# Layer two's Q and K by seven block products, one token class at a time, with the orders of four engines written out

## The chip, the cores and the metric

The kernel runs on one core of a Trainium2 chip. A core has a matrix engine (TensorE, PE in the profile), three engines that work on elements (VectorE or DVE, ScalarE or ACT, GpSimd or POOL), and a sync engine (SyncE or SP), which here issues all DMA copies. Each engine runs its own instructions in order, and an instruction that needs another engine's result waits for it; what stands behind it on the same engine waits too. Matmuls read SBUF and write PSUM, which has eight banks of 128 x 512 fp32. The metric is the device time of one execution in microseconds (us).

## The reference

Two layers, each a sliding-window attention (A) and a token-mixing MLP (B), on x of 2048 tokens x 1024 features, all in bf16:

```python
def _A_ref(x, wqkv, wo):                     # H = 32 heads of 32, W = 8, dilation 2
    qkv = ((x @ wqkv).reshape(B, S, 3, H, Dh)).transpose(2, 0, 3, 1, 4)
    q, k, v = qkv[0], qkv[1], qkv[2]
    idx = pos[:, None] - off[None, :]        # off = 0, 2, 4, ... 14
    ...
    attn = softmax(where(mask, einsum("bhsd,bhswd->bhsw", q, kg) * scale, -1e9))
    return (einsum("bhsw,bhswd->bhsd", attn, vg)...) @ wo

def _B_ref(x, w1, b1, w2, b2):
    u = gelu(einsum("bsd,sf->bdf", layernorm(x), w1) + b1)
    return (einsum("bdf,fs->bds", u, w2) + b2).transpose(0, 2, 1)

x = x + _A_ref(layernorm(x), A_wqkv, A_wo);  x = x + _B_ref(layernorm(x), ...)
x = x + _A_ref(layernorm(x), A_wqkv, A_wo);  x = x + _B_ref(layernorm(x), ...)
```

Since the dilation is 2, even and odd tokens never meet in attention. They are the two token classes, 1024 tokens each.

## The kernel before

Both layers run in one program: V for all tokens, attention with Q and K, the output projection (`out_proj`), then B's two GEMMs (`gemm1`, and `gemm2f` in layer one, `gemm2s` in layer two). In layer two, V already uses seven block products in place of eight (`Sevens`, Strassen's scheme in Winograd's form): weights and tokens are cut into 2 x 2 blocks, sums of blocks are made on DVE in fp16, and each product is four matmuls of 128 x 128 by 128 x 512 (L445). Sums between products are made by copying a PSUM bank with ACT and letting the next product add to the copy. `ahead(p, n)` hangs other work into four rounds of two token blocks each.

Attention is cut into 16 units `u` (a group of four heads, a class) and each unit into two visits of 512 tokens. Before the change both layers run the same loop (L1533): a visit issues on PE, in this order, `scores` of this visit (16 small matmuls on 32-wide tiles, one output bank for two of the four token blocks), `values` of the visit before, and two chunks of `qk_chunk` of the next unit (each 8 matmuls of 128 x 512 into an `m` bank). `in_order` fixes that order. ACT turns scores into exponentials (`pc`, L540), DVE multiplies them with the band mask into `Pm` (L552), `values` multiplies `Pm` with `v` and with ones, ACT makes the reciprocal by Ln and Exp (L588, L589), and DVE writes `oT` (L591). The keys of a unit go to `kT`; q is spread with zeros between the heads into `qB`, so that one small matmul serves four heads. ACT casts a q chunk to `qs`, and the four heads' rows go to `qB` by DVE copies (L516) or, for heads from `1 + 2n` on, by DMA from SP (L518). There are two `qB`, used in turn, and `Pm` has three slots.

The banks come from three pools: `s` has 4 banks, `m` 2 and `a` 2; scores take two `s`, values two `a`, a q or k chunk one `m`.

In the loop the weights `wqk` come in four pairs of 512 KB (`load_qk`), and in layer two DVE also takes maxima over parts of w2 (`top_load`, `top2`). `zero_p` and `zero_q` clear `Pm` and `qB` on DVE during V. In the last unit two tiles of `out_proj` a visit stand where the chunks were; a tile is two halves of 8 matmuls (L621), a residual add on DVE each (L628) with `xr`, which SP loads three ahead (`load_xr`), and the layer norm in three steps (`ln_step`).

Of the kernel before, what the change touches and what calls it, by code (L numbers as in the profile page):

```python
# [17 lines left out]
P = 128  # L18
# [10 lines left out]
def kernel(  # L29
# [135 lines left out]
    mxv = const.tile([P, 2, KD // 2], FP32, name="mxv")  # L165
    mv2 = const.tile([P, 2], FP32, name="mv2")
    csv = const.tile([P, 1], FP32, name="csv")
    civ = const.tile([P, 1], FP32, name="civ")
# [5 lines left out]
    def zero_q():  # L174
        for t in qB:
            r = nc.vector.memset(t[:].rearrange("p h t -> p (h t)"), 0.0)
        return r

    def zero_p():
        return nc.vector.memset(Pm[:].rearrange("p h t k -> p (h t k)"), 0.0)  # L180

    def zero_fill():
        zero_p()
        return zero_q()
# [4 lines left out]
    mxp = dram.tile([P, NPRE + 1], FP32, name="mxp")  # L189
    mxvd = dram.tile([P, 2], FP32, name="mxvd")  # L190
# [45 lines left out]
    def start_up(v, wv):  # L236
# [107 lines left out]
        def top_wv():  # L344
            return nc.vector.tensor_reduce(out=mv2[:], in_=mxv[:], op=ALU.max, axis=AX.X)
# [61 lines left out]
    def power_wv():  # L407
        chain_("DVE", powers, 0, 1, bcw.pop("v")[:].rearrange("p q c -> p (q c)"), csv, civ)

    class Sevens:  # L410
# [3 lines left out]
        def scale(self, j):  # L414
            w = self.wv[j][:]
            chain_("ACT", lambda: nc.scalar.activation(out=w.bitcast(FP16), in_=w, func=ACT.Identity, scale=csv[:]))
# [34 lines left out]
        def run(self, v, ahead):  # L451
# [9 lines left out]
            def put(i, r, c, src, z):  # L461
                dst = v[r][i][:, c * 512:(c + 1) * 512]
                return nc.vector.scalar_tensor_tensor(out=dst, in0=src, scalar=civ[:], in1=z, op0=ALU.mult, op1=ALU.add)

            for p in range(0, NI, 2):
# [6 lines left out]
                for i in pr:  # L472
                    in_order(self.product, bk[i][1], self.S[i][:, 0], Tn(1))
                    Z[i] = x2("z", [P, 512], FP32)
                    chain_(A, move, Z[i][:], bk[i][1], civ[:])
# [4 lines left out]
                for i in pr:  # L480
                    in_order(self.product, bk[i][0], self.a(i, 0, 1), B(1, 0), False)
                    chain_(A, move, v[0][i][:, 0:512], bk[i][0], civ[:])
# [7 lines left out]
                for i in pr:  # L490
                    in_order(self.product, bk[i][3], self.a(i, 1, 1), Tn(4), False)
                    chain_(A, move, v[1][i][:, 0:512], bk[i][3], civ[:])
# [34 lines left out]
    def scores(u, b):  # L527
        q, k = qB[u % 2], kT[u % 2]
        s0 = (2 * u + b) % NS * HB
# [8 lines left out]
        pc = pcp.tile([P, HB, HG, GW], BF16, name="pc", tag="pc")  # L538
        for n in range(2):
            nc.scalar.activation(out=pc[:, 2 * n:2 * n + 2].rearrange("p t h k -> p (t h k)"), in_=ss[n][:, 0:2 * HG * GW],  # L540
                                 func=ACT.Exp, scale=scale, bias=shift[:])
        exps[:] = pc, s0
# [3 lines left out]

    def mask(*rs):
        pc, s0 = exps
        for r in rs:
            rp = slice(r * KG, (r + 1) * KG)  # L550
            mk = band[rp].unsqueeze(1).unsqueeze(1).to_broadcast([KG, HB, HG, GW])
            mm = nc.vector.tensor_tensor(out=Pm[rp, :, s0:s0 + HB, r * KG:r * KG + GW].rearrange("p h t k -> p t h k"),  # L552
                                    in0=pc[rp], in1=mk, op=ALU.mult)
        return mm

    def values(u, b, v, oT):
        g, c = divmod(u, DIL)
# [23 lines left out]
        for lo_, n_, t_ in runs:  # L581
            for h in range(HG):
# [3 lines left out]
                                      skip_group_check=True)  # L586
        rd = x2("rd", [P, 512], FP32)
        nc.scalar.activation(out=rd[:], in_=acc[1][:], func=ACT.Ln)  # L588
        nc.scalar.activation(out=rd[:], in_=rd[:], func=ACT.Exp, scale=-1.0)  # L589
        lo = c * SC + t0 * P  # L590
        norm.append(lambda: nc.vector.tensor_tensor(out=oT[g][:, lo:lo + HB * P], in0=acc[0][:], in1=rd[:], op=ALU.mult))  # L591
        return mm

    norm = []
# [213 lines left out]
    def top_load(k):  # L808
        t = wt_("w2p", [P, 8, 256])
        pre[k] = t  # L810
        for n in range(2):
            i, f = divmod(2 * k + n, NB2)
            r = nc.sync.dma_start(out=t[:, 4 * n:4 * n + 4], in_=w2_v[:, 4 * f:4 * f + 4, i * 256:(i + 1) * 256])
        return r

    def top2(k, j):
        i, f = divmod(4 * k + j, 2 * NB2)
        return nc.vector.tensor_reduce(out=mx2[:, i, f:f + 1], in_=pre[k][:, 2 * j:2 * j + 2, :], op=ALU.max, axis=AX.XY,
                                       apply_absolute_value=True)

    pre = {}

    def gemm1(h2, g, first):
# [115 lines left out]
        for fb in range(1, NFB):  # L939
# [59 lines left out]
            if not first and fb == 2:  # L999
                share_w2(0, 2 * NB2)  # L1000
            if not first and fb == 5:
# [180 lines left out]
    def gemm2f(g, src, dst, seam):  # L1182
# [180 lines left out]
        t2(*range(4))  # L1363
        normalise(0, 1)
# [31 lines left out]
        for i in range(2, NI):  # L1396
# [55 lines left out]
            if i + 2 < NI:  # L1452
                load_w(i + 2)
                if i == 3:
# [46 lines left out]
    for li in range(2):  # L1501
        first = li == 0
        v = [[None] * NI for _ in range(DIL)]
        for c, i in order:
            v[c][i] = vhp.tile([P, D], BF16, name="v", tag="vh")
        if first:
# [3 lines left out]
            res = lambda c, i: xin_v[c, i]  # L1510
        else:
            def ahead(p, n):
                if p == 0 and n == 0:
                    rest()
                elif p == 2 and n == 0:
                    chain_("DVE", zero_p)
                elif p == 4 and n == 0:
                    chain_("DVE", zero_q)
                elif n and p + 2 < NI:
                    for m in range(4):  # L1520
                        for k in range(2):
                            sv[0].s_sum(p + 2 + k, m)

            sv[0].run(v, ahead)
            res = lambda c, i: rows(xb, c, i)
        oT = [gop.tile([P, S], BF16, name="oT", tag="go") for _ in range(NG)]
        h2 = [[None] * NI for _ in range(DIL)]
        chunks = [(0, 0), (0, 1), (1, 0), (1, 1)]
        if first:
            last_pe[0] = None  # L1530
        for part, n in chunks:
            in_order(qk_chunk, 0, wts, part, n)
        for vis in range(2 * NU):  # L1533
            u, b = divmod(vis, 2)
            if first and vis == 5:
                chain_("SP", keep_wv)
            if b == 0 and u % (2 * DIL) == 1 and u + 3 < NU:
                nxt = [None, None]
                chain_("SP", load_qk, u // (2 * DIL) + 1, nxt)
            if b == 0 and (u + 1) % (2 * DIL) == 0 and u + 1 < NU:  # L1540
                wts = nxt
            if vis == 2 * NU - 8:
                wo = []
                chain_("SP", load_wo, wo)
            if vis == 2 * NU - 3:
                todo[:] = order
                for _ in range(3):
                    load_xr(res)
            if vis % 4 == 0 and vis < 4 * (DIL * NPRE if first else NB2):
                chain_("SP", pre_load if first else top_load, vis // 4)  # L1550
            in_order(scores, u, b)
            if u + 1 < NU:
                mask(0, 1, 2, 3)
            else:
                chain_("DVE", mask, 0, 1)
            if vis:
                in_order(values, *divmod(vis - 1, 2), v, oT)
                if u + 1 < NU:
                    divided = norm.pop()()
                else:  # L1560
                    chain_("DVE", norm.pop())
            k, j = divmod(vis - 3, 4)
            if 0 <= k < (DIL * NPRE if first else NB2):
                with tc.issue_after(divided.ins):
                    (pre_top if first else top2)(k, j)
            if first and vis == 2 * NU - 4:
                bc0 = pre_share()
            for n in range(2):
                if u + 1 < NU:
                    in_order(qk_chunk, u + 1, wts, *chunks[2 * b + n])  # L1570
                    continue
                half, add, store, ln = out_proj(0, 2 * b + n, oT, wo, res, xa[li], h2)
                in_order(half, 0)
                chain_("DVE", add, 0)
                if n == 0:
                    chain_("DVE", mask, 2, 3)
                else:
                    ln_step()
                in_order(half, 1)
                chain_("DVE", add, 1)  # L1580
                store()
                lns.append(list(ln))
                if n:
                    ln_step()
        in_order(values, NU - 1, 1, v, oT)
        if first:
            chain_("DVE", power, 0, 1 + NPRE, bc0[:].rearrange("p q b -> p b q"))
        for k, (c, i) in enumerate(order[4:]):
            if k in (8, 10):
                chain_("SP", load_w1, k // 2 - 4)  # L1590
# [24 lines left out]
        wv, wts = [], [None, None]  # L1615
# [41 lines left out]
```

## Time and profile before

| | us |
|---|---|
| runs (three) | 1199.63, 1200.66, 1204.48 |
| median | 1200.66 |
| the profiled execution's own time | 1200.14 |
| its span | 1198.4 |
| layer one, attention with Q and K (PE L505) | 62.6 to 203.1 |
| layer two, V (L447) | 607.9 to 656.4 |
| layer two, attention with Q and K | 656.4 to 797.4 |
| layer two, rest of attention and output projection | 797.4 to 861 |
| layer two, first GEMM from block 1 on | about 872 to 1029 |

Busy us in three of these windows:

| window | PE | DVE | ACT | POOL | DMA, GB/s |
|---|---|---|---|---|---|
| 62.6 to 203.1 | 140.5 | 110.2 | 96.2 | 0 | 79 |
| 607.9 to 656.4 | 48.5 | 30.3 | 25.7 | 0 | 33 |
| 656.4 to 797.4 | 140.3 | 112.2 | 96.4 | 0 | 81 |

Times in a table or in a profile line are us from the start of the span; the span runs from the first to the last instruction, and the profiled execution's own time has a little more around it. In a line of the timeline the first number is the start, the second how long the group took, and `x16` the number of instructions in it; in a line of a group the last numbers are busy time and the mean of one in ns, and after the second bar the idle time before them.

### The profile page before, as it was taken

The numbers are of one execution on the slowest core, as the hardware profiler recorded it, in microseconds if no ns is written. First come the engines' busy times: TensorE is split into PE (matmuls) and PEld (weight loads), VectorE is DVE, ScalarE is ACT, GpSimd is POOL, SyncE is SP. The second block draws the span as 40 slices with busy tenths as digits, with TensorE's granted clock in tenths as the row PEclk, the third lists the DMA queues.
The fourth block names the chain that finished last, engine by engine and source line by source line (L and its number), as shares of the span: only waits on it lengthen the run. The fifth ranks groups of instructions, "written<-read, shape, count | busy, mean of one in ns | idle before, by whom it ended". The sixth has DMA issues, their size and how long they took to land.

```text
span 1198.4 us, 20518 instructions
## 1 busy us (share of the span) xinstructions
PE 1191.6 (99%) x7972; PEld 548.5 (46%) x7972; DVE 780.6 (65%) x1513; ACT 692.9 (58%) x1164; POOL 125.6 (10%) x121
## 2 busy tenths in 40 slices
PE   9999999999999999999999999999999999999998
PEld 4444444444444444444444444444444444444444
DVE  7558887887777546957665788888612221874663
ACT  5757676578777777665744677654544434432342
POOL 0000000281000031000000000003911212100000
PEclk9999999999999999999999999999999999999999
DMA  8922233696676778975510232435855645175521
GB/s 238 158 63 71 72 109 94 207 284 176 183 222 180 211 198 190 219 186 147 177 43 19 68 85 71 121 98 176 263 161 164 202 146 168 41 193 141 156 73 36
DMA packets 248561, 174.12 MB, mean 145 GB/s; under 512 B 48400, under 2 KB 224784, under 8 KB 245136
## 3 DMA queue, kind: packets, MB, share of 16 engines
q1 hardware_dynamic: 248464, 172.82, 52.3%
q8 instruction: 62, 1.02, 0.4%
q14 instruction: 35, 0.29, 0.1%
HBM read 130.30 MB, written 30.43 MB: 134 GB/s over the span
## 4 chain that ended last, share of the span: by engine, by line
PE 97%; DMA 1%; ACT 1%; DVE 0%; issue 0%; DVEq 0%
PE m L505 19%; PE s L876 11%; PE m L621 9%; PE m L876 7%; PE s L1080 7%; PE a L876 6%; PE s L1230 5%; PE m L1080 4%; PE s L297 3%; PE a L1080 3%; PE m L1230 3%; PE s L702 2%; PE s L536 2%; PE s L447 2%; PE s L1323 2%; PE a L1230 2%
## 5 line engine op out<-in xcount | busy, mean ns | idle before, releaser
L505 PE MATMUL m<-hT,wqk 128*128 128x512 bf16 x1024 | 231.8, 380 | 0.0
L552 DVE TENSOR_TENSOR Pm<-pc,band 32x640 bf16<-32x640 bf16 x256 | 123.5, 483 | 45.6 <-ACT pc L540 38.8
L505 PEld LDWEIGHTS <-wqk 128*128 128x128 bf16 x1024 | 95.3, 98 | 117.9 <-issue 10.7
L876 PEld LDWEIGHTS <-Sw 128*128 128x128 f16 x832 | 81.4, 98 | 98.7 <-issue 0.7
L621 PE MATMUL m<-wo,oT 128*128 128x512 bf16 x512 | 111.8, 379 | 0.0
L876 PEld LDWEIGHTS <-w 128*128 128x128 f16 (+1 forms) x624 | 61.1, 98 | 73.6
L716 POOL TENSOR_TENSOR T<-h 128x512 f16<-128x512 bf16 x16 | 18.4, 1152 | 606.4 <-DMA xr<-xb 357.5
L621 PEld LDWEIGHTS <-oT 128*128 128x128 bf16 x512 | 49.6, 98 | 60.6 <-issue 1.9
L716 DVE TENSOR_TENSOR py<-pz,m 128x512 f32<-128x512 f32 x14 | 9.6, 688 | 91.2 <-PE m L876 62.8
L540 ACT ACTIVATE pc<-s,shift 128x320 bf16<-128x320 f32 x128 | 60.9, 532 | 11.6 <-PE s L536 11.6
L876 PE MATMUL s<-T,Sw 128*128 128x512 f16 x288 | 66.2, 379 | 0.4 <-ACT s L885 0.4
L512 ACT CAST qs<-m 128x512 bf16<-128x512 f32 x64 | 37.5, 586 | 44.3 <-PE m L505 41.2
L509 ACT CAST kT<-m 128x512 bf16<-128x512 f32 x64 | 37.5, 586 | 41.8 <-PE m L505 38.8
L716 POOL TENSOR_TENSOR Pm<-g 128x512 f16<-128x512 bf16 x24 | 28.6, 1208 | 282.5 <-ACT Pm L797 163.7
L628 DVE TENSOR_TENSOR xn<-m,xr 128x512 bf16<-128x512 f32 x64 | 44.1, 689 | 15.2 <-PE m L621 15.0
L661 ACT ACTIVATE h<-xn,bi,rs 128x1024 bf16<-128x1024 bf16 x32 | 39.7, 1240 | 23.1 <-DVE bi L647 23.1
L876 PE MATMUL a<-h,w 128*128 128x512 bf16 x224 | 52.9, 379 | 0.0
L876 PE MATMUL m<-T,Sw 128*128 128x512 f16 x224 | 52.9, 379 | 0.0
L852 ACT ACTIVATE w<-w,cs 128x2048 f16<-128x2048 bf16 x26 | 51.8, 1997 | 0.0
L1080 PEld LDWEIGHTS <-u 128*128 128x128 f16 x336 | 32.9, 98 | 39.6
L516 DVE COPY qB<-qs 32x512 bf16<-32x512 bf16 x136 | 38.2, 281 | 18.5 <-ACT qs L512 15.5
L716 DVE TENSOR_TENSOR xs<-tq,xs 128x512 bf16<-128x512 f32 (+1 forms) x30 | 21.9, 733 | 43.2 <-ACT tq L1235 26.1
(251 smaller groups left out, 2183.6 us busy)
## 6 DMA issues: line engine op xcount, KB each, us to landing
w<-in_B_w_dram SPq DMA_DIRECT2D x110, 512.0 KB, 6.1
sd<-Sw SPq DMA_DIRECT2D x13, 1024.0 KB, 8.3
Sw<-sd SPq DMA_DIRECT2D x13, 1024.0 KB, 4.9
wqk<-in_A_wqkv_dram SPq DMA_DIRECT2D x16, 512.0 KB, 5.0
xa<-xn SPq DMA_DIRECT2D x32, 256.0 KB, 3.2
xs<-xa SPq DMA_DIRECT2D x32, 256.0 KB, 3.4
Pm<-in_B_w_dram SPq DMA_DIRECT2D x26, 256.0 KB, 6.4
wo<-in_A_wo_dram SPq DMA_DIRECT2D x8, 512.0 KB, 5.8
```

Source lines behind the costliest of these rows:

```text
L505: mm = nc.tensor.matmul(ps[:], lhsT=wts[part][:, kt, (g % 2) * P:(g % 2 + 1) * P], rhs=hT[:, kt, lo:lo + 512], start=(kt == 0), stop=(kt = ...
L516: nc.vector.tensor_copy(out=qB[u % 2][hp, h, ls], in_=qs[hp, :])
L540: nc.scalar.activation(out=pc[:, 2 * n:2 * n + 2].rearrange("p t h k -> p (t h k)"), in_=ss[n][:, 0:2 * HG * GW], func=ACT.Exp, scale=scal ...
L552: mm = nc.vector.tensor_tensor(out=Pm[rp, :, s0:s0 + HB, r * KG:r * KG + GW].rearrange("p h t k -> p t h k"), in0=pc[rp], in1=mk, op=ALU.mult)
L621: mm = nc.tensor.matmul(ps[:], lhsT=oT[g][:, cols(c, i)], rhs=wo[n][g // 4][:, g % 4, :], start=(g == 0), stop=(g == NG - 1))
L628: return nc.vector.tensor_tensor(out=xn[:, xs_], in0=pss_["o", n][:], in1=xr[:, xs_], op=ALU.add)
L661: last["ACT"] = nc.scalar.activation(out=h2[c][i][:], in_=xn[:], func=ACT.Identity, bias=t["bi"][:], scale=t["rs"][:])
L716: return eng.tensor_tensor(out=out, in0=a, in1=b, op=op)
L852: return nc.scalar.activation(out=w[:].bitcast(FP16), in_=w[:], func=ACT.Identity, scale=cs[:, fb + 1:fb + 2])
L876: r = nc.tensor.matmul(out, lhsT=lhs[:, k, :], rhs=rhs[k], start=start and k == 0, stop=stop and k == NI - 1, skip_group_check=True)
L1080: r = nc.tensor.matmul(out, lhsT=lhs[k], rhs=rhs[k][:, cols_], start=start and k == 0, stop=k == K - 1, skip_group_check=True)
L1230: r = nc.tensor.matmul(out, lhsT=lhs[k], rhs=rhs[k], start=start and k == 0, stop=k == K - 1, skip_group_check=True)
```

## The change

Layer one keeps its loop, with one addition: after every second visit ACT takes a sum of absolute values over half a `wqk` tile (`bound_qk`), 16 in all, from which a scale for the fp16 weights of Q and K follows (`mxq`, then `mv2`, `csv` and `civ`, which now have two columns). The step that sends these to DRAM (`keep_wv`) moves from layer one's attention into `gemm2f`.

Layer two gets two classes. `QkBlocks` works during V: it loads the weights of two head groups at a time (512 KB, k or q), scales them on ACT, makes the four weight sums on DVE, and writes both to DRAM (`sdq`). The clearing of `Pm` and `qB` moves from DVE to GpSimd. `Attention` then runs cycles `p` = 0 to 7, and a remainder as cycle 8. A cycle makes k and q of two head groups of one class by seven products each and does the four visits of the cycle before. All of class 0 comes first (`by_class`). Products 1 and 5 take an `s` bank each, the two banks that are copied on an `m` bank each. The order of each engine is a list; `-` means an item of the cycle before, and `cycle` only interleaves the four lists so that each item's needs come earlier.

```diff
+    def by_class(u):
+        p = u // 2
+        return 2 * (p % (NG // 2)) + u % 2, p // (NG // 2)
+    class QkBlocks:
+        def load(self, n):
...
+            chain_("SP", lambda: nc.sync.dma_start(out=self.R[n][:], in_=wq_v[:, :, lo:lo + 256]))
+        def scale(self, n):
+            t = self.R[n][:]
+            chain_("ACT", lambda: nc.scalar.activation(out=t.bitcast(FP16), in_=t, func=ACT.Identity, scale=csv[:, 1:2]))
+        def sums(self, n):
...
+            for o, x, y, op in ((q[0], a21, a22, ALU.add), (q[1], q[0], a11, ALU.subtract), (q[2], a11, a21, ALU.subtract),
+                                (q[3], a12, q[1], ALU.subtract)):
+                chain_("DVE", tt, nc.vector, o, x, y, op)
+        def keep(self, n):
...
+            chain_("SP", lambda: nc.sync.dma_start(out=sdq[n][0], in_=r[:].bitcast(FP16)))
+            chain_("SP", lambda: nc.sync.dma_start(out=sdq[n][1].rearrange("p k c -> p (k c)"), in_=t[:].rearrange("p a k c -> p (a k c)")))
+    class Attention:
+        NP = 4 * NG // 4
+        PE = "P1k P4q- P5k S1 P6k V1 P2k P7k S2 P3k V2 P4k P1q P5q S3 P6q V3 P2q P3q S4 P7q V4"
+        ACT = ("x4- abk c21q- e1a e1b pck l1 x1 Zk c11k e2a e2b l2 x2 abq c21k e3a e3b pcq l3 x3 Zq c11q e4a e4b l4")
+        DVE = ("m40- n4- m41- m42- m43- m10 m11 m12 m13 n1 y22k y12k m20 m21 m22 n2 m23 t1 m30 m31 m32 m33 n3 y12q y22q t2")
+        SP = "dc21q- wk wq dy12q dc11q dy22q"
...
+            return {"S": [("e" + o + "a", d), ("e" + o + "b", d), ("dc11q", p - 1), ("dy12q", p - 1)]
+                    + ([("dc21q", p - 1), ("dy22q", p - 1)] if c in "34" else []),
...
+        def cycle(self, p):
+            qs = {}
+            for e in ("PE", "ACT", "DVE", "SP"):
+                q = [(n[:-1], p - 1) if n.endswith("-") else (n, p) for n in getattr(self, e).split()]
+                qs[e] = [x for x in q if self.there(*x) and not (p == self.NP and x[1] == p)]
+            while any(qs.values()):
...
+        def do(self, n, p):
+            x, k, f = self.x, n[:-1], n[-1]
+            if n[0] == "d":
+                a, b = {"11": (0, 0), "12": (0, 1), "21": (1, 0), "22": (1, 1)}[n[2:4]]
+                for h in range(HG):
+                    hp = slice(h * DH, (h + 1) * DH)
+                    chain_("SP", lambda: nc.sync.dma_start(out=qB[a][hp, h, b * 512:(b + 1) * 512], in_=self.qs[hp, 2 * a + b]))
+                return
...
+                if k in ("ab", "pc"):
+                    o, i = ("pb", "pa") if k == "ab" else ("pc", "pb")
+                    bk[o] = bank("m")
+                    return nc.scalar.copy(out=bk[o][:], in_=bk[i][:])
+                if k == "Z":
+                    bk["z"] = x2("z", [P, 512], FP32)
+                    return nc.scalar.activation(out=bk["z"][:], in_=bk["pd"][:], func=ACT.Identity, scale=ci_)
...
+                return nc.vector.scalar_tensor_tensor(out=dst, in0=bk["pc" if a else "pb"][:], scalar=ci_, in1=bk["z"][:],
+                                                      op0=ALU.mult, op1=ALU.add)
```

The letters: `P1k` to `P7q` are products, `ab` and `pc` the copies from bank to bank, `Z` the scaled copy of product 5, `c11`, `c21`, `y12`, `y22` the four finished 128 x 512 blocks (c on ACT, y on DVE), `dc11q` and the like the four DMA copies that take one finished block of q to `qB`; `S`, `e`, `m`, `V`, `l`, `x`, `n` are scores, exponentials, mask, values, Ln, Exp and the division; `wk` and `wq` load the weights of a later cycle (two copies of 512 KB each), `t` a token sum. DVE no longer writes `qB`. Keys have four buffers in place of two.

The driver of layer two:

```diff
+            oT = [gop.tile([P, S], BF16, name="oT", tag="go") for _ in range(NG)]
+            at.start(v, oT, wo)
+            at.load(2)
...
+            at.cycle(0)
...
+            for p in range(1, at.NP):
+                at.cycle(p)
+            todo[:] = order
+            for _ in range(3):
+                load_xr(res)
+            at.cycle(at.NP)
+            ahead_tiles = 7
+            plan = [1, 2, 2, 1, 1]
...
+            for vis in range(2 * NU - 4, 2 * NU):
+                in_order(scores, *divmod(vis, 2))
                 chain_("DVE", mask, 0, 1)
                 in_order(values, *divmod(vis - 1, 2), v, oT)
+                chain_("DVE", norm.pop())
+                for n in range(plan[vis - 2 * NU + 5]):
+                    last_tile(k, n)
+                    k += 1
```

So one tile of `out_proj` comes before the last four visits, and 2, 2, 1 and 1 tiles follow these; each `last_tile` of layer two does two `ln_step`s. The maxima over parts of w2 move from attention into the second layer's `gemm1`, blocks 1 to 7, with two loads of 256 KB and two reductions of 128 x 1024 on DVE a block.

## The prediction

> **What bounds it now.** I read the page first: shares, then the chain that ended last.
>
> ```profile
> PE 1191.6 (99%) x7972; PEld 548.5 (46%) x7972; DVE 780.6 (65%) x1513; ACT 692.9 (58%) x1164; POOL 125.6 (10%) x121
> ...
> PE 97%; DMA 1%; ACT 1%; DVE 0%; issue 0%; DVEq 0%
> ...
> L505 PE MATMUL m<-hT,wqk 128*128 128x512 bf16 x1024 | 231.8, 380 | 0.0
> ```
>
> TensorE is never without work, so time is TensorE time: taking matmuls away pays in full, and any new TensorE wait costs in full. Half of L505's 1024 matmuls belong to layer two, which the change rewrites. So I read the timeline of layer two's attention for the price of each kind of TensorE work.
>
> ```profile
> 608.07 1.03 PE L447 MATMUL a<-wv,hT 128*128 128x512 f16 x4
> ...
> 656.42 7.07 PE L505 MATMUL m<-hT,wqk 128*128 128x512 bf16 x32
> 663.42 0.46 PE L536 MATMUL s<-qB,kT 128*32 128x160 bf16 x16
> 663.81 3.63 PE L505 MATMUL m<-hT,wqk 128*128 128x512 bf16 x16
> ...
> 672.66 3.63 PE L505 MATMUL m<-hT,wqk 128*128 128x512 bf16 x16
> 676.22 0.46 PE L536 MATMUL s<-qB,kT 128*32 128x160 bf16 x16
> 677.08 3.63 PE L505 MATMUL m<-hT,wqk 128*128 128x512 bf16 x16
> ...
> 805.31 7.08 PE L621 MATMUL m<-wo,oT 128*128 128x512 bf16 x32
> 812.32 0.19 PE L568 MATMUL a<-Pm,v 128*32 128x8 bf16 x4
> 812.93 32.33 PE L621 MATMUL m<-wo,oT 128*128 128x512 bf16 x149
> ```
>
> The V stage does 224 matmuls from 608.07 to 656.42: 0.216 us each, in groups of four too. A row's last big matmul starts at its start + (count-1) x 0.216; from there to the next big one, less 0.216, is what small-tile work costs. Scores alone: 663.81 - (656.42 + 31 x 0.216) - 0.216 = 0.48. Scores and values together: 677.08 - (672.66 + 15 x 0.216) - 0.216 = 0.96. Values alone: 812.93 - (805.31 + 31 x 0.216) - 0.216 = 0.70. So apart they cost 1.18, together 0.96: each time the array passes between big and small tiles it pays, about 0.21 more for a visit whose scores and values are split.
>
> Last, how q reaches qB: the same timeline for SP's queue, qB's own view, and the DMA issues.
>
> ```profile
> 666.36 2.44 SPq L518 DMA_DIRECT2D qB<-qs  x4
> ...
> 675.21 2.41 SPq L518 DMA_DIRECT2D qB<-qs  x4
> ...
> L518 SPq DMA_DIRECT2D qB<-qs x120: 507/543/1640, 72.8 to 793.0; - x120
> ...
> DMA to landing us min/median/max: 1.8/1.8/5.7
> ...
> xr<-xb SPq DMA_DIRECT2D x16, 256.0 KB, 2.9
> ```
>
> Issuing one copy occupies SP 0.54 us, and four take 2.44, so they stand (2.44 - 0.54)/3 = 0.63 apart; each lands 1.8 after its issue. Before, VectorE wrote a part of qB (L516), and one chunk sent at most four copies.
>
> **The change on TensorE.** (a) 16 units x 4 chunks x 8 = 512 matmuls become 8 cycles x 2 x 7 x 4 = 448: 64 x 0.216 = **-13.8**. (b) A cycle's list puts a product between every scores and values (S1 P6k V1 ...), where visits had them side by side. 27 values lose their neighbour: 27 x 0.21 = **+5.7**. A cycle is then 56 x 0.216 + 4 x (0.48 + 0.69) = 16.8 us against 4 x (16 x 0.216 + 0.96) = 17.7.
>
> **(c) The wait for q.** S1 of a cycle reads all heads of c11q and eight columns of y12q, made in the cycle before. Nothing but DMA writes qB now: SP issues dy12q and dc11q, eight copies, and S1 needs the last. Counted from the start of P3q: its result can be read 1.07 later (608.07 to the ACT read at 609.14), DVE still finishes masks and n3 for some 0.2, y12q takes 0.75 (row L463): 2.1. Eight copies: 0.05 + 7 x 0.63 + 1.84 = 6.3; weights and entry 0.1. S1 can start at 8.5. TensorE has P3q, S4, P7q, V4, P1k, P4q, P5k before it: 5 x 0.864 + 0.48 + 0.69 = 5.5. So TensorE stands **3.0 us** once a cycle, and with it everything behind S1 in its order: P6k, V1 and the rest; ACT and DVE starve with it. S2 to S4 come later than their copies. Six cycles: 18.0. The first wait is longer: cycle 0 has no S4 and V4 (1.2 less cover), and copies wait for the landing of the copy eight places before, which here are weight loads (0.8, from walking the queue): 5.0. Together **+23.0**. Bounds: issues 0.55 apart (the closest in the trace) give -0.6 a cycle, -4 in all; copies landing after 3.7 (seen just before a load) give +1.9, +13 in all.
>
> **(d) Other waits inside a cycle.** ACT holds 4 copies (0.57), 6 scalings (0.69), 8 exps (0.42 apart), 4 pairs of 1.24: 14.7 of 16.8 us; DVE 16 masks (0.51), 4 normalisations (0.61), 4 y (0.67): 13.3; SP 16 x 0.63 + 4 loads: 12.5. P6k follows P1k by 2.2 and needs 1.07 + 0.57 = 1.7; P7 and P4 come with similar room. Only cycle 0, without scores and values between, shows waits (P4k and P4q for y22): **+0.6**, bounds 0 to 2.
>
> **(e) The end.** Scores of visit 28 wait as S1 does, but behind P4q and a tile (16 x 0.216): +1.0. The first tile's residual loads xr stand on SP behind twelve qB copies (7.5 us) and take 2.9 to land; its adds hold both m banks, so the second tile waits: about +3.5. Then visits 28 to 31 carry 2, 2, 1, 1 tiles and two LN steps in each: DVE has 4 x (2.04 + 0.61) for masks and divisions and six tiles at 2.8: 27.4 us, TensorE 6 x 3.46 + 4 x 0.96 = 24.6: +3.0. **+7.5**, bounds 0 to 10. Before, TensorE did not wait here.
>
> **At nothing.** In layer one, 16 maxima of 1.07 + 0.19 (row L341) on ACT; ACT is busy 96 of 140 us there, and one late cast would delay scores by less than 1 us. In V: 8 scalings of 1.9 on ACT (25.7 busy of 48.5), 32 sums of 0.33 and 16 T sums of about 0.65 on DVE (30.3 busy, of which 6.3 of zeroing moves to POOL, idle there; 14.8 K elements a partition at 1.2 us per 512, the dearest POOL row, are 35 us: done before the first q copy near 668). The maxima of w2 move into the second layer's GEMM (14 x about 1.2 on DVE, 37 busy of 157; their 14 copies of 256 KB go with them, SP issues one per 0.6 and the x2 buffers they take are free again after one maximum). keep_wv's one copy moves to the first layer's second GEMM, block 2; it lands in 2.9 (mxvd), and the weight scale is wanted three blocks later. The V stage's DMA is a rival below.
>
> **Sum.** -13.8 + 5.7 + 23.0 + 0.6 + 7.5 = +23.0. The profiled execution took 1200.14 (span 1198.4, 1.7 around it); the median of runs is 0.5 higher. 1200.14 + 23.0 gives 1223.1; I say **1223.5**.
>
> **Rivals.** *The wait is covered* (not slower). It decides when the eight copies land within 3.3 us of y12q; with 1.84 of landing that asks for issues 0.2 apart, where no row is below 0.55, or for scores that need fewer copies, which the built order does not show. Then (c), S28 and xr fall away: 1200.1 - 13.8 + 5.7 + 0.6 + 3.0 = 1195.6, within 0.5%.
>
> *The clock falls.* At the kernel's start the same 128x512 matmul runs slower:
>
> ```profile
> 1.05 4.02 PE L318 MATMUL s<-warm 128*128 128x512 bf16 x9 [1.05 <-DVE warm L111]
> ```
>
> That is (4.02 - 0.61)/8 = 0.43 apart for some 4 us. If a wait of 3 us brought that back, 4 us at half speed lose 2.0, seven times: 1237. Against it: TensorE's longest gap so far, 1.24 us at 599.0, left the granted clock at 1.00; a longer one no row shows. The Trainium skill, page "TensorE: Matmul & The Clock Gate", "What's actually happening", says that a free-running window of about 3.4 us without work halves the clock. By that rule, waits of 3.0 are just too short and the first, 5.0, is long enough in about half the cases: +1.
>
> *The DMA of the weights.* V's stage gains 4 MB of loads, 8 MB written back and 5 MB read again between 608 and 673: 260 GB/s, where 797 to 861 moved 227 at a busy share of 0.71 (320 if full). At 220 it ends 12 us late and cycle 0's products wait: about +10, 1233.
>
> That fewer products are built than said is excluded: the built order holds 448.
>
> **Chances.** Forecast 0.72, weights' DMA 0.10, clock 0.08, covered 0.07, the rest 0.03 (other waits either way). From the bounds: low 1223.5 - 4 - 7.5 = 1212, high the clock's 1237 with 2 more; 1211 to 1239 leaves out the covered case, half of the clock's and late copies. A measurement here tells about 0.5% (6 us) from no change: slower 0.92, same 0.05, faster 0.03.
>
> **What would show it.** Products x448 at 0.216. Scores waiting for DMA qB about 3 us once every 19.8 us, seven times; SP's copies 0.63 apart in runs of 12 or more. A cycle of 16.8 with no such wait refutes (c). A granted clock under 1 between 660 and 800 speaks for the clock; a long wait of the first products on the weights (Aq, Bq) for the DMA. In the end, waits of TensorE on xn's adds; if tiles follow each other without gaps, (e) is wrong.

## The result, and the profile after

| | median us | lowest to highest | runs |
|---|---|---|---|
| before | 1201.85 | 1199.63 to 1204.48 | 6 |
| changed | 1236.7 | 1233.62 to 1399.39 | 6 |

The changed kernel is slower: the ratio is 1.0283, interval 1.0262 to 1.0304. Its highest time, 1399.39, is that of its profiled execution, which was disturbed (a granted clock of 0.85 on the mean) and is left out of the ratio (the median of the other five is 1236.18); so the lines below come from the same kernel run once more, the first experiment (e1: 1239.11 us, span of the profile 1236.5).

First the page of e1: busy time, granted clock in 40 slices, and the chain that ended last by engine.

```profile
PE 1187.2 (96%) x7774; PEld 543.2 (44%) x7908; DVE 802.1 (65%) x1509; ACT 733.7 (59%) x1220; POOL 138.3 (11%) x124
...
PEclk9999999999999999999999899999999999999999
...
PE 85%; DMA 6%; DVE 3%; ACT 2%; issue 2%; SPq 1%; DVEq 0%; ACTq 0%
```

TensorE's share of the chain fell from 97% to 85%, and DMA's rose from 1% to 6%. Before, the clock's row held only nines. What TensorE waited for, all over the program (us in total, times, longest):

```profile
PE s L778 <- DMA qB<-qs: 22.4, 7, 6.6
PE m L891 <- DVE xn L898: 4.9, 3, 4.2
...
PE s L1133 <- ACT s L1142: 2.2, 1, 2.2
```

L778 is the scores' matmul, L891 that of `out_proj`. The first profile of the kernel before has neither of the first two lines. One cycle of layer two on TensorE, and the queue of SP beside it (start, duration, then the instructions that stand together):

```profile
700.12 1.03 PE L640 MATMUL s<-Tq,Bq 128*128 128x512 f16 x4
703.82 0.46 PE L778 MATMUL s<-qB,kx 128*32 128x160 bf16 x16 [2.67 <-DMA qB<-qs]
704.21 1.89 PE L640 MATMUL m<-Tq,Bq 128*128 128x512 f16 x4
...
708.21 1.03 PE L640 MATMUL m<-Tq,Bq 128*128 128x512 f16 x4
```

```profile
697.43 10.80 SPq L655 DMA_DIRECT2D qB<-qs  x16
```

The scores S1 stand 2.67 us for q's copies, while SP issues sixteen of them in a row, (10.80 - 0.5)/15 = 0.69 us apart. The four matmuls behind the wait take 1.89 us where four take 1.03 elsewhere: TensorE came back at half speed.

So where did the time go? The program is cut at the start of the first Q/K product of layer two and at the start of the last matmul of the first MLP block (L702 before, L972 in e1):

| profile | V of layer two starts | first Q/K product | block's last matmul | attention and projection | rest |
|---|---|---|---|---|---|
| before | 608.1 | 656.4 | 868.0 | 211.6 | 330.5 |
| before, again (e5) | 614.2 | 662.6 | 873.8 | 211.2 | 330.5 |
| changed (e1) | 612.9 | 662.1 | 905.9 | 243.8 | 330.6 |

The loss is in the third stage, 32.4 us against the mean of the two profiles before. V takes 0.8 us longer, and the rest is the same. Layer one differs more between the two profiles of the unaltered kernel (6.1 us) than between e1 and either (4.8 and 1.3); e5 comes back to that.

### The profile page after: what moved, and what is told of

Its sections match the earlier page's. It is cut to its first block, busy times and chain, and to the rows that moved or that the text cites. A ratio compares the mean times of both kernels' runs of the same rounds, so it can differ in the third digit from the quotient of the medians.

```text
span 1397.2 us, 20558 instructions
## 1 busy us (share of the span) xinstructions
PE 1358.4 (97%) x7774; PEld 583.5 (42%) x7908; DVE 801.5 (57%) x1509; ACT 741.5 (53%) x1220; POOL 137.2 (10%) x124
## 4 chain that ended last, share of the span: by engine, by line
PE 94%; DMA 3%; SPq 1%; issue 1%; ACT 1%; DVE 0%; DVEq 0%; ACTq 0%
PE s L1133 12%; PE m L741 9%; PE m L891 9%; PE m L1133 8%; PE s L1342 7%; PE a L1133 6%; PE s L1492 5%; PE m L640 4%; PE m L1342 4%; PE s L299 3%; PE a L1342 3%; PE m L1492 3%; PE s L640 2%; PE s L972 2%; PE a L1492 2%; PE s L449 2%
## 5 line engine op out<-in xcount | busy, mean ns | idle before, releaser
L1133 PEld LDWEIGHTS <-Sw 128*128 128x128 f16 x832 | 88.3, 106 | 120.5
L891 PE MATMUL m<-wo,oT 128*128 128x512 bf16 x498 | 129.7, 425 | 5.2 <-DVE xn L898 3.9
L741 PE MATMUL m<-hT,wqk 128*128 128x512 bf16 x481 | 128.4, 421 | 3.6 <-issue 2.2
L891 PEld LDWEIGHTS <-oT 128*128 128x128 bf16 x512 | 53.8, 106 | 78.1 <-issue 7.9
L741 PEld LDWEIGHTS <-wqk 128*128 128x128 bf16 x512 | 51.0, 104 | 71.4 <-issue 6.3
L1133 PE MATMUL s<-T,Sw 128*128 128x512 f16 x288 | 76.4, 422 | 0.0
L1133 PE MATMUL m<-T,Sw 128*128 128x512 f16 x224 | 61.0, 423 | 0.0
L1133 PE MATMUL a<-h,w 128*128 128x512 bf16 x218 | 59.5, 422 | 0.5
L986 DVE TENSOR_TENSOR py<-pz,s 128x512 f32<-128x512 f32 x12 | 8.2, 687 | 79.1 <-PE s L1133 66.1
L1133 PE MATMUL s<-h,w 128*128 128x512 bf16 x186 | 50.8, 423 | 0.5
L853 DVE TENSOR_TENSOR oT<-a,rd 128x512 bf16<-128x512 f32 x64 | 44.2, 691 | 10.3 <-ACT rd L848 8.8
```

The source lines that it names most:

```text
L741: mm = nc.tensor.matmul(ps[:], lhsT=wts[part][:, kt, (g % 2) * P:(g % 2 + 1) * P], rhs=hT[:, kt, lo:lo + 512], start=(kt == 0), stop=(kt = ...
L853: return nc.vector.tensor_tensor(out=oT[g][:, lo:lo + HB * P], in0=acc[0][:], in1=rd[:], op=ALU.mult)
L891: mm = nc.tensor.matmul(ps[:], lhsT=oT[g][:, cols(c, i)], rhs=wo[n][g // 4][:, g % 4, :], start=(g == 0), stop=(g == NG - 1))
L986: return eng.tensor_tensor(out=out, in0=a, in1=b, op=op)
L1133: r = nc.tensor.matmul(out, lhsT=lhs[:, k, :], rhs=rhs[k], start=start and k == 0, stop=stop and k == NI - 1, skip_group_check=True)
```

## The experiments

Each experiment is compared with runs of the kernel before on the same chip, whose median was 1203.83 us for e1 to e4, 1203.93 for e5 to e8, 1205.89 for e9 and e10, and 1200.67 for e11. The stage is attention and projection of the table above. "Half clock" is the time in that stage with a granted clock of 0.50, "waits" are TensorE's waits there for q (its copies, or `qs`) and for xn. Stage, half clock and waits come from the one profiled execution, which is not always near the median: e7's took 1204.48, 5.4 below it, and e10's 1204.64, 4.2 above.

| | median us | ratio to before, interval | stage | waits, q and xn | half clock |
|---|---|---|---|---|---|
| e1, the changed kernel | 1239.11 | 1.0300 (1.0283 to 1.0318) | 243.8 | 22.4 + 4.9 | 27.3 |
| e2, long fill | 1238.08 | 1.0286 (1.0271 to 1.0301) | 240.3 | 2.6 + 4.9 | 6.8 |
| e3, q first | 1207.92 | 1.0034 (1.0021 to 1.0047) | 212.8 | 3.2 + 1.1 | 6.8 |
| e4, xr early | 1235.37 | 1.0261 (1.0243 to 1.0279) | 240.5 | 23.0 + 1.1 | 27.3 |
| e6, small fill | 1230.93 | 1.0215 (1.0195 to 1.0234) | 237.5 | 7.4 + 5.6 | 6.8 |
| e7, side by side | 1209.89 | 1.0039 (1.0020 to 1.0057) | 212.9 | 8.2 + 1.1 | 6.8 |
| e8, no maxima | 1210.99 | 1.0056 (1.0041 to 1.0071) | 213.3 | 9.8 + 1.1 | 3.4 |
| e9, two queues | 1212.81 | 1.0058 (1.0044 to 1.0073) | 216.6 | 7.0 + 1.1 | 6.8 |
| e10, ordered | 1200.45 | 0.9956 (0.9941 to 0.9971) | 207.8 | 5.2 + 1.1 | 3.4 |
| e11, both | 1191.13 | 0.9920 (0.9907 to 0.9934) | 201.9 | 0.2 + 1.1 | 0 |

**e1, the changed kernel again.** No edit.

> The changed kernel, unaltered, to see its profile at an undisturbed clock. Theory W (waits alone, as forecast): seven waits of scores for the q copies, the first about 5 us, the others about 3.0, cycles of 19.8 us, granted clock 1.00 throughout, total 1223 to 1227. Theory C (waits and a clock that falls after them, the rival priced at 1237): waits of 2.5 to 3 us, and products in the cycles further apart than 0.216 us for some us after each wait, granted clock in the cycles clearly under 1, total 1234 to 1238.

Measured: 1239.11, 12 us above the span of theory W and 1 us above that of theory C, whose signs are all there (the kernel before, too, was 2 us slower on this chip than the 1201.85 above). In the cycles six waits of 2.6 to 2.7 us and a first one of 6.6 are followed, five times out of seven, by a stretch of granted clock 0.50 that lasts 3.4 us or twice that. The clock of the whole span, 0.988, hides this: only a cut into short windows shows it.

**e2, long fill.** Work that keeps the clock up, in the place of the wait: 16 matmuls of zeros ahead of S1 in each cycle, into the bank that the scores then overwrite.

```diff
+        for _ in range(fill):
+            nc.tensor.matmul(ss[0][:].rearrange("p (n q) -> p n q", q=P), lhsT=warm[:],
+                             rhs=warm[:].unsqueeze(1).to_broadcast([P, 4, P]), start=True, stop=True)
```

> Sixteen matmuls of zeros (3.46 us at 0.216) stand ahead of the scores of each cycle's first visit and write a scores bank that the scores then overwrite; TensorE works where it waited for q. Theory W: nothing is gained, since the work only fills the wait: 0.5 us more per cycle, total about 3 us above the changed kernel. Theory C: the clock stays at 1.00 in the cycles and the total falls, although TensorE has 112 matmuls more, to about 1226 (1236.7 less the 13 us above the forecast, plus 3).

Measured: 1238.08, neither. The half clock behind the waits went (6.8 us are left, at the end), but 16 matmuls take 3.5 us and the wait they were to fill 2.7, so in six cycles they held the scores up themselves (in the first, 2.6 us of its longer wait were left). The stage did fall by 3.5 us, for which theory W has no reason; the time hardly shows it, since layer one took 4.2 us longer in e2's profile than in e1's (V of layer two from 617.1 and 612.9). An experiment that takes one cost away and brings in another of the same size tells little by its time; e6 mends this.

**e3, q first.** Q's products before K's in every cycle, so that q's copies have half a cycle more to land:

```diff
-        PE = "P1k P4q- P5k S1 P6k V1 P2k P7k S2 P3k V2 P4k P1q P5q S3 P6q V3 P2q P3q S4 P7q V4"
+        PE = "P1q P4k- P5q S1 P6q V1 P2q P7q S2 P3q V2 P4q P1k P5k S3 P6k V3 P2k P3k S4 P7k V4"
...
-        SP = "dc21q- wk wq dy12q dc11q dy22q"
+        SP = "dc21q- dy22q- wk dc11q dy12q wq"
```

ACT's and DVE's lists change in the same way. K goes to `kT` and `kx` with no copy behind.

> In every cycle q's seven products come first and k's second; the q copies of tokens 0 to 511 follow the second scores, those of the rest follow the fourth, so they have half a cycle to land. The same products, copies and element work. Theories W and C both: the waits of scores for q vanish from the second cycle on, cycles of about 16.8 us, clock 1.00, and the total falls by the waits and what the clock lost: to 1199 to 1203 (1200.1 - 13.8 + 5.7 + 0.6 + 2 for the first cycles + 4 to 6 at the end). A rival, that SP's queue or the element engines bound the cycle: cycles stay at 18 us or more, total above 1212.

Measured: 1207.92, 31 us less than e1 on the same chip; the stage fell by 31.0 as well. Its waits:

```profile
PE s L778 <- DMA qB<-qs: 3.2, 2, 2.9
...
PE m L891 <- DVE xn L898: 1.1, 2, 0.6
```

So the order in which q and k are made, not the products or the amount of copying, costs nearly all of the loss. That the time is 5 us above what was expected has two parts: the first cycle still waits (2.9 us, and 6.8 of half clock behind it), and the expectation went from a profile whose layer one was 5.7 us faster than e3's (V of layer two from 608.1 and 613.8).

**e4, xr early.** The three residual loads go in front of the last cycle:

```diff
             for p in range(1, at.NP):
+                if p == at.NP - 1:
+                    todo[:] = order
+                    for _ in range(3):
+                        load_xr(res)
                 at.cycle(p)
-            todo[:] = order
-            for _ in range(3):
-                load_xr(res)
```

> The first three residual loads are issued before cycle 7 in place of after it, so they no longer stand behind twelve q copies. If term (e) of the forecast is right, TensorE's wait of 3 to 4 us for the first residual adds vanishes and the total falls by about 3.5 us; if the copies' place on SP is not the cause, nothing changes.

Measured: 1235.37, 3.7 less than e1. The wait of 4.2 us for xn is gone, 1.1 is left. The half clock at the end went with it, but two more windows of it came behind the waits of the last cycles, so that its sum stayed at 27.3.

**e5, the kernel before again.** No edit.

> The kernel before, unaltered, with a second profile. It tells whether the five microseconds that layer one lost in every profile of the changed kernel (its V of layer two starts at 612.9 to 617.1, and at 608.1 in the first profile of the kernel before) are the change's. Theory L: layer one's DMAs of weight maxima (bc from mxd) land at times that differ from run to run, and a late one stalls TensorE in gemm1 near 410; then this profile too can show V of layer two starting at 610 or later. Rival M: the changed kernel's layer one is slower by itself, through the maxima of wqk that ACT now takes in attention; then this profile starts V of layer two at 608 within 1 us, and no TensorE wait over 1.5 us near 410.

Measured (one run, 1205.99 us): V of layer two starts at 614.2. Theory L holds: the same wait is in the unaltered kernel. The row on TensorE's timeline:

```profile
415.54 3.09 PE L876 MATMUL s<-T,Sw 128*128 128x512 f16 x7 [2.67 <-ACT s L885]
```

In the first profile this wait was 0.4. ACT stands there behind a gelu, that behind DVE's scale for the weights, and that behind the broadcast `bc` of the maxima, for which DVE stood 2.0 us here and not at all in the first profile. So the baseline has a wait near 412 that is sometimes hidden and sometimes not, with half clock behind it (seven matmuls in 3.09).

**e6, small fill.** As e2, with 8 matmuls in each cycle and 24 in the first.

> The changed kernel with 8 matmuls of zeros (1.7 us at full clock) ahead of the scores that wait for q once a cycle, and 24 of them (5.2 us) in the first cycle. They lie inside the waits, so the copies of q still set when the scores start. Theory C, the waits cost themselves and also bring half-clock spells of 3.4 us behind them, worth up to 1.7 us each: no wait is left over about 2 us in the cycles, the granted clock stays at 1.00 from 660 to 820, and the time is 7 to 9 us below the changed kernel's, 1229 to 1232. Theory W, only the waits cost and the excess over the forecast lies elsewhere: 1237 to 1240, clock or not.

Measured: 1230.93, inside theory C, 8.2 us below e1 (the kernel before took about 1203.9 beside both). TensorE in the cycle that was shown of e1:

```profile
697.18 1.03 PE L640 MATMUL s<-Tq,Bq 128*128 128x512 f16 x4
698.04 1.89 PE L774 MATMUL s<-warm 128*128 128x512 bf16 x8
700.89 0.54 PE L781 MATMUL s<-qB,kx 128*32 128x160 bf16 x16 [0.95 <-DMA qB<-qs]
701.36 1.04 PE L640 MATMUL m<-Tq,Bq 128*128 128x512 f16 x4
```

The scores start no sooner after P5k (700.89 - 697.18 = 3.71; in e1 703.82 - 700.12 = 3.70), but the four matmuls behind them now take 1.04 where they took 1.89. The wait costs the same; the half clock behind it was a cost of its own.

**e7, side by side.** On e3's order: values right behind scores, for the visit two back, so that masks are ready; P6 ahead of S1; the first cycle's q copies ahead of its weights; xr as in e4.

```diff
-        PE = "P1q P4k- P5q S1 P6q V1 P2q P7q S2 P3q V2 P4q P1k P5k S3 P6k V3 P2k P3k S4 P7k V4"
+        PE = "P1q P4k- P5q P6q S1 V1 P2q P7q P3q S2 V2 P4q P1k P5k P6k S3 V3 P2k P7k P3k S4 V4"
...
-            vis = 4 * (p - 1) + int(n[1]) - 1 - (n[0] in "Vlxn")
+            vis = 4 * (p - 1) + int(n[1]) - 1 - 2 * (n[0] in "Vlxn")
```

> Q's products ahead of K's as in e3, scores and values side by side again (values of the visit two back, so that their masks are ready), the first cycle's q copies ahead of its weight loads, the first residual loads before the last cycle. Term (b) of the prediction says that side by side saves 27 to 28 times 0.21, 5.7 to 5.9 us, against e3's 1207.9, and the first cycle's wait with its half-clock spell (about 2.9 + 1.7) goes too: 1198 to 1201. Rival: splitting scores and values costs nothing in fact, the array's change between big and small tiles being hidden; then 1203 to 1205.

Measured: 1209.89, a miss: no better than e3. New waits had come, eight for `qs`. TensorE's waits, and then what one of the DVE instructions that it waited for stood for itself:

```profile
PE m L642 <- DVE qs L694: 8.2, 8, 3.3
```

```profile
698.01 0.75 DVE L694 SCALAR_TENSOR_TENSOR qs<-m,civ,z 128x512 bf16<-128x512 f32 x1 [1.02 <-DMA qB<-qs]
```

y22q of this cycle overwrites a part of `qs` that the copies of the cycle before still read. These copies are the last four of eight on SP. The same copies that e3 took off the scores' path were now late for the next writer of their source.

**e8, no maxima.** As e7, with the bound on wqk set to a constant in place of ACT's 16 maxima in layer one.

> As e7, without the 16 maxima of wqk on ACT in layer one: the bound for Q's and K's weight scale is a constant, set once. Rival M (the maxima delay layer one): the first product of V in layer two starts 4 to 5 us sooner than in e7, at about 608, and the time is 4 to 5 us below e7's. Theory L (run-to-run timing of DMAs in gemm1): within 2 us of e7, with the start of V anywhere from 608 to 617.

Measured: 1210.99, 1.1 us above e7, V from 613.4 (610.0 in e7). The maxima cost nothing that can be seen beside the 6 us by which runs of one kernel differ here.

**e9, two queues.** The changed kernel, with half of q's copies issued by POOL:

```diff
-                    chain_("SP", lambda: nc.sync.dma_start(out=qB[a][hp, h, b * 512:(b + 1) * 512], in_=self.qs[hp, 2 * a + b]))
+                    e, q = ("POOL", nc.gpsimd) if n[1] == "y" else ("SP", nc.sync)
+                    chain_(e, lambda: q.dma_start(out=qB[a][hp, h, b * 512:(b + 1) * 512], in_=self.qs[hp, 2 * a + b]))
```

> The changed kernel with the copies of y12q and y22q issued by POOL, which has nothing else to do in this stage, so that SP issues four copies of q instead of eight ahead of the waiting scores. Theory S, the wait of 3.0 us is eight issues in line on one queue (7 x 0.63) and then a landing: if POOL issues a copy in up to about 0.9 us and lands it like SP's, the scores can start some 2 us sooner, the waits of the six cycles fall from 3.0 to 0.5 to 1.0, the half-clock spells behind them go, and the time is 1213 to 1220. Rival Q: the copies are late for another reason (the DMA engines, the landing itself), or POOL issues much slower: waits of 2.5 us and more remain and the time is 1232 or more.

Measured: 1212.81, just under theory S: the waits of the six cycles are gone whole, and the first, 6.4, remains. The wait for xn fell to 1.1 as well, which the expectation hadn't counted: its loads now stand on SP behind fewer copies. Waits of TensorE, then POOL's queue:

```profile
PE s L779 <- DMA qB<-qs: 7.0, 2, 6.4
```

```profile
698.90 3.91 POOL L656 DMA_DIRECT2D qB<-qs  x8 [19.36 <-DVE qs L693]
715.83 3.91 POOL L656 DMA_DIRECT2D qB<-qs  x8 [13.02 <-DVE qs L693]
```

POOL issues a copy every (3.91 - 0.50)/7 = 0.49 us, and a cycle without a wait takes 715.83 - 698.90 = 16.9 us. It was the line of eight issues on one queue that made the scores late.

**e10, ordered.** e7 with y22q's copies ahead of c21q's, the first cycle's weights loaded before the last weight sums are kept, and xr before cycle 6:

```diff
-        SP = "dc21q- dy22q- dc11q dy12q wk wq"
+        SP = "dy22q- dc21q- dc11q dy12q wk wq"
```

> As e7, with what its profile showed late put right: the copies of y22q go ahead of those of c21q (y22q of the next cycle waited for them to read qs: 8.2 us of TensorE waits in eight places, two of them followed by half clock), the first cycle's weight loads are issued before the last weight sums are kept, and the residual loads stand before cycle 6 in place of cycle 7. If side by side is worth its 5.9 and e7 lost it to these waits, then most of 8.2 plus 2 to 3 of half clock comes back: 1198 to 1202, against 1203.9 for the kernel before. Rival: other waits take their place, and the time stays at 1206 or more.

Measured: 1200.45, inside the expected span, and a ratio below one for the first time. e7's 8.2 us of waits for `qs` became 4.1. By the profiles the stage gave back 5.1 us; the medians differ by 9.4, but they come from two chips, and e7's profile is that of its quickest execution.

**e11, both.** The orders of e10 with the two queues of e9.

> The orders of e10 and the two queues of e9 together. e10's profile still has 5.2 us of TensorE waits for q's copies (one of 2.1 is followed by 3.4 us of half clock, up to 1.7 us more); with the copies on two queues they should land some 2 us sooner and these waits go: 5 to 7 us below e10, a ratio of 0.990 to 0.993 to the kernel before. Rival: the waits left are not from the copies' issue; within 2 us of e10, ratio 0.994 to 0.998.

Measured: 1191.13. The ratio is in the expected span; the 9.3 us below e10 are more than expected, but that compares two chips (by the stages it is 5.9). Of the waits for q, 0.2 us is left in the whole stage, and no half clock. This version beats both kernels: 0.9920 of the kernel before (0.9907 to 0.9934).

## Why the prediction was right, and where it was not

Slower was right and the time lies inside the range, but the likeliest value, 1223.5, is 13 us too low; 1.2 of these are the kernel before itself (1201.85 here, 1200.66 when the sum was made). The time is inside the range only because the range's upper end was set by the clock rival's 1237. Point by point, for the stage's 32.4 us:

*(a) 64 matmuls fewer.* Held: e9's profile has 448 of them, and their spacing at full speed is 0.216 (rows of four start 0.86 apart).

*(b) Split values, +5.7.* Held. Some matmuls are missing from most profiles; e9's is complete around a scores and a values that stand apart, and e10's around a pair side by side:

```profile
696.69 1.03 PE L640 MATMUL m<-hT,Bq 128*128 128x512 bf16 x4
697.64 0.46 PE L779 MATMUL s<-qB,kT 128*32 128x160 bf16 x16
698.03 1.04 PE L640 MATMUL m<-Tq,Bq 128*128 128x512 f16 x4
699.00 0.42 PE L828 MATMUL a<-Pm,v 128*32 128x136 bf16 x16
...
699.58 1.04 PE L640 MATMUL s<-hT,Aq 128*128 128x512 bf16 x4
```

```profile
703.24 1.03 PE L642 MATMUL m<-Tq,Bq 128*128 128x512 f16 x4
704.19 0.46 PE L780 MATMUL s<-qB,kx 128*32 128x160 bf16 x16
704.48 0.41 PE L829 MATMUL a<-Pm,v 128*32 128x136 bf16 x16
...
705.05 1.04 PE L642 MATMUL s<-hT,Aq 128*128 128x512 bf16 x4
```

Scores alone: 698.03 - 696.69 - 4 x 0.216 = 0.48; values alone: 699.58 - 698.03 - 0.86 = 0.69; both together: 705.05 - 703.24 - 0.86 = 0.95. Apart they cost 0.22 more, 27 times: 5.9. e7 gained this and lost as much to `qs`.

*(c) The wait for q, +23.0.* 22.4 were measured. The place and the cause (e9) are as predicted. That the sum came so near is in part luck, since its parts miss in opposite directions: six waits are 2.6 to 2.7 in place of 3.0, and the first is 6.6 in place of 5.0. There SP sent the first copy at 673.67, right behind y12q, but the fifth to the eighth each waited for a weight load issued eight places before to land (SP's queue, 664 to 686):

```profile
SPq L655 <- DMA Aq<-sdq: 1.5, 2, 1.1
SPq L655 <- DMA Bq<-sdq: 1.4, 2, 0.7
```

That is the mechanism of the prediction, with 2.9 us where it put 0.8. Two queues don't help here: in e9 the first wait is still 6.4.

*(d) Waits inside a cycle, +0.6.* About 0.5 for y22, and 1.0 for masks near the end.

*(e) The end, +7.5.* 4.9: the wait for xn is 4.9 (predicted 3.5, and 3.0 for DVE's layer norm, of which little came), and the scores of visit 28 didn't wait. e4 shows the cause: loading xr early gives back 3.7.

*"Any new TensorE wait costs in full."* This was the step that failed, and with it the sentence that set the clock aside, "waits of 3.0 are just too short". The other ground against the clock, a gap of 1.24 us at 599.0, was misread: 1.24 is how long that row's matmuls took, and the idle time before them is 0.86.

```profile
599.01 1.24 PE L1230 MATMUL m<-Pm,qa 128*128 128x512 f16 x5 [0.86 <-ACT m L1235]
```

A wait cost more than in full. In e1's stage the clock was at 0.50 for 27.3 us; TensorE stood still for 5.6 of these, and in the other 21.7 it did half the work: 10.9 us lost. The stage then adds up: -13.8 + 5.9 + 22.4 + 4.9 + 1.5 + 10.9 = 31.8, where 32.4 was measured. e6 takes away the clock's part alone, for the five stretches in the cycles: 20.5 us with 3.8 of standing in them, 8.4 by the same working. The medians of e1 and e6 differ by 8.2. That this comes so near is in part chance: the stages of the two profiles differ by 6.3, and 1.2 more went to e6's zeros and waits (72 x 0.216 + 7.4 + 5.6 = 28.6 in place of 22.4 + 4.9 = 27.3).

The rival that was given 0.08 is therefore what happened, beside the likeliest case and not in place of it: it priced seven drops at 2.0, and six came, five behind the scores' waits and one behind xn, for 10.9 in all. What makes a drop can be read off by cutting e1 where the half-clock stretches begin. All seven lie on one grid, n x 3.413 us apart (414.1, 680.3, 704.2, 724.7, 765.6, 786.1, 830.5). Three pairs of neighbouring windows of that grid (stretch, its length, then busy time of PE and other engines; PEclk is the third number from the end):

```profile
410.70:414.10 3.40, 1.19 (x7) 0.48 (x5) 3.30 (x10) 2.11 (x4) 0.00 (x0) 1.00 0.93 329
414.10:417.50 3.40, 3.40 (x9) 1.22 (x9) 2.31 (x4) 2.25 (x2) 0.00 (x0) 0.50 0.92 278
700.80:704.20 3.40, 0.73 (x18) 0.29 (x16) 1.19 (x3) 0.22 (x2) 0.00 (x0) 1.00 0.18 48
704.20:707.60 3.40, 3.07 (x44) 1.43 (x39) 1.93 (x4) 1.86 (x4) 0.00 (x0) 0.50 0.18 46
741.70:745.10 3.40, 1.57 (x8) 0.49 (x6) 2.23 (x5) 1.38 (x3) 0.00 (x0) 1.00 0.18 48
745.10:748.50 3.40, 2.39 (x50) 1.29 (x52) 1.14 (x3) 1.96 (x4) 0.00 (x0) 1.00 0.21 56
```

The wait before 745.95 is as long as the one before 703.82 (2.68 and 2.67), but it falls across the border of two windows: 1.57 us of work in the first are enough, and no drop follows. In the windows 700.80 and 410.70 there was work for 0.73 and 1.19 us only, and the next window is at half clock. The profiles of ten runs (e1 to e10) were cut in this way, into 3451 windows that began at full clock, from 20 us to the last whole window but one: in 26 of them TensorE stood still for 2.04 us or more, and the next window was at half clock each time; in the other 3425 it stood still for 1.91 or less (25 of these over 1.0), and the clock stayed. What decides is thus the standing time inside one window of a fixed grid, about 2 us of 3.41, not a wait's whole length. What ends a drop is open: 8 of the 34 windows at half clock were followed by another one, with 0.64 to 3.19 us of standing in them, while one with 0.84 was not. A wait of 2.65 us puts 2 us or more into one window for (3.41 - 2.65) + 2 x (2.65 - 2.0) = 2.06 us of the 3.41 at which it may begin, six times in ten if it begins anywhere alike; four of six did.

The Trainium skill, page "TensorE: Matmul & The Clock Gate", section "What's actually happening", gives the window as 3413 ns, free-running, and the half clock "after ≥1 idle window (~3.4µs)". The trace agrees with the window and with its not starting anew at a wait; it differs on how idle a window must be. The prediction read the rule as a whole window, by which only the first wait could count.

*"At nothing."* The maxima in layer one (e8), the work in V (0.8 us longer) and the maxima of w2 (rest of 330.6 against 330.5) held. The rival of the weights' DMA fell: no TensorE wait for Aq or Bq appears.

*The baseline.* The sum started from one profiled execution of 1200.14. e5 shows that the start of layer two's V differs by 6 us between executions of the kernel before, 4 of them through the wait near 412 (2.3 longer) and the half-clock window behind it (1.7), 1.0 within the first 63 us and 0.5 in a wait near 395; the rest was not traced. That the forecast named no such thing didn't hurt it, since both kernels share it, but it is of the size of the 0.5% that this measurement can tell.

What was argued and not tried: why `bc` lands at different times in layer one, and the first cycle's wait in the changed kernel taken away alone (e7, e10 and e11 do so among other edits).

## What to carry to other kernels

Where TensorE is the bound, price a new wait twice: its length, and half of the window at half clock that follows (or of two) if 2 us or more of standing time fall into one window of 3.41 us; several short waits, or a little work in the middle of a long one, cost less than one long wait. Where a consumer needs many small copies, count the issues in line on their queue ahead of the last one it needs: here eight in a line cost more than the products saved, and an idle engine's second queue, or making the copied operand first, gave the time back. When copies are moved off one path, look at who overwrites their source next.

## What the runs showed of the hardware that was not expected

The granted clock of TensorE falls to 0.50 after a window of 3.413 us on a fixed grid in which it stood still for 2.04 us or more (26 of 26), and not after 1.91 or less (3425 of 3425). In the half-clock windows a 128x512 matmul follows the other after 0.43 us instead of 0.216.

POOL's queue, which the kernel before had not used for a copy, issued a copy of q in 0.50 us (median of 64 in e9), SP in 0.58 (median of 64 in the same profile).
